# Another hand-written order for the first steps of a fused chunked attention and spatial-gating MLP

## The chip, the cores and the metric

The kernel runs on one core of one Trainium2 chip, in one launch. The metric is device time in microseconds (us), the median of several runs. The core has five engines that run side by side, each in its own program order: TensorE (PE, matmuls and transposes), VectorE (DVE), ScalarE (ACT), GpSimd (POOL) and SyncE (SP), which here only issues DMAs. In the profile PEld is PE's loading of weights.

## The reference

Four sequences (B = 4) of 768 tokens with 8 heads of 64 go through two blocks, everything in float32.

```python
# attention, per chunk of 32 queries; 8 memory keys, 16 keys to the left, 8 to the right
k_full = concat([mem_k, k[c_start-16 : c_end+8]]);  v_full likewise
a = softmax(q_c @ k_full.T / 8)
out[c] = a @ v_full
x = out as [B, 768, 512]
# gated MLP
h = gelu(x @ w_in)                      # w_in 512 x 1024
u, v = h[..., :512], h[..., 512:]
v_n = (v - mean(v)) / sqrt(var(v) + 1e-6) * g_ln
v_s = einsum('ts,bsd->btd', w_sg, v_n) + b_sg
out = x + (u * v_s) @ w_out
```

## The kernel before

The work is cut into 24 attention units (unit u is 128 tokens of one sequence, six units to a sequence) and, for each sequence, into MLP products. Large products take each operand as a high and a low part, so that one product is three groups of matmuls (`product`).

Every piece of work is a named step, and the string `ORDER` lists the steps. A loop goes through `ORDER` and lets each step issue its instructions. Since each engine keeps program order, `ORDER` is, read engine by engine, the queue of that engine; waits between engines follow from the data. Most steps run on a fixed engine; some can run on either of two, and a `*` behind the name takes the second one.

The names that matter here, with unit or part number behind them:

- `q`, `k`, `v`: loads of a unit's queries (256 KB, two buffers qa, qb), keys (368 KB, two buffers ka, kb) and values (512 KB, three buffers). A load into a buffer that an earlier unit used waits on SP until that unit's matmuls have read it, and everything behind it in SP's order waits too. `q2` and `k2` so wait for `S0`, `q3` and `k3` for `S1`, `q4` and `k4` for `S2`, `q5` and `k5` for `S3`, `q6` and `k6` for `S4`.
- `S`: 64 small matmuls for a unit's scores, into one PSUM tile `s` that all units share. `mx`, `sb`, `sm`, `sr` (DVE): row maximum, subtraction (which frees `s`), sum, reciprocal. `ex` (ACT): exponential. `nm` (DVE, `*` POOL): division, into the one tile `na`. `z`: clears what lies outside the sequence (POOL). `T`: four PE transposes of `na`; `p` (ACT, `*` DVE) copies them to SBUF as `pt`. `A`: 64 small matmuls with the values into one PSUM tile `av`. `xc`, `xh` (ACT) and `xl` (POOL or DVE): the result, its high and its low part.
- `ri13`, `ri12` and so on: loads of an eighth of w_in as raw 64-bit words (512 KB; raw buffers a to f). `d1` to `d6` decode them to float32 and split them: `d1` ACT, `d2` DVE (`*` ACT), `d3` and `d4` DVE, `d5` ACT (high part), `d6` POOL (`*` DVE, low part). `cb` loads g_ln and b_sg. `g`, `ga`, `gb`: load, high part, low part of a piece of w_sg; `ro` a quarter of w_out.
- `V`, `U`, `W`, `O`: the MLP's products on PE. `Va`, `Vb` are halves of a `V` for the first three units; `Vb00` needs `ri12`, `ri13` decoded and unit 0's high and low part. `v1` to `v9`, `u1` to `u4`, `w1` to `w4`, `o1` are the engines' work behind them.
- `zz4`: four matmuls of `ident` by `ident` into a free PSUM tile, whose result nobody reads. Each float32 matmul of `zz` shows as two MATMUL records, so `zz4` is eight, `zz1` two.

PE's order before begins: zz4 S0 S1 zz1 T0 S2 A0 S3 zz2 zz3 T1 zz1 Vb00 T2 S4 A1 Va00 T3 A2 Vb01 Va01 Vb02 S5 A3 T4. SP's order before begins: q1 q0 k0 k1 ri13 ri12 q2 k2 v0 ri11 q3 k3 q4 ri10 ri01 k4 v1 ri00 v2 ri02 cb k5 q5 v3 q6 k6 ri03.

Of the kernel before, what the change touches and what calls it, by code (L numbers as in the profile page):

```python
# [33 lines left out]


ORDER = """
zz4 q1 q0 k0 k1 S0 mx0 sb0 ex0 z0 sm0 sr0 nm0* S1 zz1 ri13 ri12 d1i12 d2i13* d1i13 q2 k2 mx1 sb1 T0 S2 ex1 v0
ri11 q3 k3 d2i12 d3i12 d4i12 sm1 d3i13 d5i12 p0 A0 mx2 sr1 sb2 nm1 d4i13 d6i12 S3 zz2 zz3 q4 ri10 ri01 k4 v1
T1 d2i11* d1i11 xh0 d3i11 d4i11 d5i13 ex2 d6i13 d5i11 xl0 mx3 sm2 sb3 sr2 nm2 zz1 Vb00 T2 S4 ri00 d6i11 d1i10
d2i10* ex3 p1 d2i01* xc0 d3i10 d4i10 A1 d3i01 d5i10 d1i01 d6i10 v2 ri02 cb k5 q5 v3 q6 k6 ri03 Va00 d2i00* xc1  # L40
xh1 d1i00 v100 sm3 sr3 p2* mx4 d3i00 d4i01 xl1* nm3* d4i00 v200 T3 A2 d5i01 xh2 sb4 xl2 d1i02 v300 d2i02* ex4
v400 sm4 v500 sr4 d3i02 vx00 Vb01 Va01 Vb02 xc2 p3 d5i00 v101 d6i01 cbh S5 v201 mx5 d6i00* sb5 A3 nm4* vy00
v600 T4 zz1 xc3 xh3 ex5 v301 d1i03 d2i03* p4* d4i02 z5 v401 sm5 d3i03 v700 v800 xl3 Va02 U001 S6 V03 d4i03
v900* mx6 v501 d5i03 u1001 v102 d5i02 v202 sb6 d6i03 d6i02 q7 k7 v4 g51 g11 g10 g21 q8 g20 g40 v302 u2001 sr5
u3001 ex6 vx01 nm5 vy01 v601 z6 A4 ga10 S7 xh4 ga21 ga51 u4001 mx7 v402 xl4 v701 ga20 v801 gb20* v502 sm6 sr6
gb21* vx02 U002 T5 p5 ga40 xc4 gb10 v901 v103 vy02 nm6* ga11 u1002 v203 u2002 v303 U003 u1003 u3002 sb7 v403
u4002 v503 v602 gb51 v702 gb40* V04 k8 q9 v5 A5 ex7 vx03 u2003 vy03 v603 S8 T6 g01 k9 ro0 ga01 xh5 p6 xl5
u3003 v802 v703 v803 v902 U000 V05 v903 xc5 v104 u4003 sm7 mx8 sb8 v204 gb01* sr7 v6 g50 S9 A6 g31 k10 q10
v105 ex8 nm7* gb11 ga31 gb31 v205 ga50 v305 gb50 d2o0 v405 g41 v7 v304 v404 g30 k11 U012 T7 sm8 mx9 v505 v504
sr8 vx05 u1000 ga41 gb41 p7 xc6 u1012 u2000 sb9 u3000 u2012 vx04 u4000 u3012 g00 v8 q11 U011 A7 S10 u4012 mx10  # L50
vy05 nm8* v605 ga30 v705 vy04 v604 T8 U013 U010 ga00 xc7 d3o0 v704 gb30* v804 v904 v805 ex9 d1o0 gb00* p8*
sb10 A8 S11 v905* sm9 u1010 u2010 u3010 u1011 ex10 d4o0 mx11 u2011 u4010 u3011 sm10 sr9 u4011 v9 q12 ro1 k12
k13 d2o1* d1o1 W001 d3o1 w1001 w2001 ro2 d5o0 W003 w1003 q13 W000 d4o1 d6o0* nm9* w2003 w1000 sb11 W002 w2000
sr10 d2o2 d3o2 w3003 ex11 d1o2 S12 w4003 w3001 xc8 w4001 z11 v10 ro3 v11 d4o2 w1002 w2002 d5o2 u1013 w3002
# [591 lines left out]
```

## Time and profile before

| | |
|---|---|
| median of 3 runs | 382.08 us (379.43 to 382.45) |
| profiled execution, its own time | 382.09 us |
| its span, first to last instruction | 380.3 us |
| PE busy | 365.1 us, 96% of the span |
| DVE, ACT, POOL busy | 254.2, 152.5, 120.1 us |
| DMA | 47.65 MB, mean 125 GB/s |

The profiled execution is as long as the median, and 1.8 us of it lie outside the span. Busy time says how long an engine had an instruction in it; what sets the end is read from the chain of waits and from the engines' timelines.

### The profile page before, as it was taken

To read this page: it belongs to the slowest core of one execution; us is meant where nothing else is said; L and a number is where in the kernel's file an instruction comes from. 1 tells how busy PE (TensorE), PEld (TensorE's weight loads), DVE (VectorE), ACT (ScalarE), POOL (GpSimd) and SP (SyncE) were. 2 spreads that over 40 slices of the span, in tenths; PEclk is the share of its full clock that TensorE was granted. 3 is DMA by queue.
4 is the path that set the end of the run, shared out by engine and by line. 5 is a ranking of instruction groups with operands and counts; after the bars stand their busy time and mean duration, and the time that the engine had idled before them with its cause. 6 is when DMAs were issued, how large, how long until landed. Compare 5 with 4: busy or idle time off the path is not lost.

```text
span 380.3 us, 11104 instructions
## 1 busy us (share of the span) xinstructions
PE 365.1 (96%) x4804; PEld 342.3 (90%) x4804; DVE 254.2 (67%) x472; ACT 152.5 (40%) x292; POOL 120.1 (32%) x144
## 2 busy tenths in 40 slices
PE   3698899999999999999999999999999999999996
PEld 3598788999998998899999888999999888999995
DVE  1988899997877868874545678766573347743642
ACT  1677686664314254540312254541221255531200
POOL 0255275622230333441402134731023055520210
PEclk9999999999999999999999999999999999999999
DMA  7998785845244533515111453204202300000033
GB/s 250 349 302 280 248 276 172 293 162 184 94 164 149 164 82 95 215 47 191 22 51 38 144 163 123 71 9 121 100 0 91 119 9 0 3 0 2 0 111 118
DMA packets 24528, 47.65 MB, mean 125 GB/s; under 512 B 4384, under 2 KB 13600, under 8 KB 24480
## 3 DMA queue, kind: packets, MB, share of 16 engines
q1 hardware_dynamic: 24480, 46.94, 37.4%
q8 instruction: 38, 0.62, 0.6%
q14 instruction: 10, 0.08, 0.1%
HBM read 36.96 MB, written 6.29 MB: 114 GB/s over the span
## 4 chain that ended last, share of the span: by engine, by line
PE 94%; DVE 3%; DMA 1%; issue 1%; SPq 0%; ACT 0%; POOL 0%; DVEq 0%
PE mmd L106 23%; PE mmc L106 22%; PE mma L106 21%; PE mmb L106 17%; PE av L106 7%; PE s L106 5%; DMA ka<-in_ks 1%; DVE ea L106 0%; DVE exc L106 0%; DVE rda L106 0%; SPq L106 0%; DVE rdb L106 0%; DVE mxa L106 0%; DVE mc L106 0%; DVE eb L106 0%
## 5 line engine op out<-in xcount | busy, mean ns | idle before, releaser
L106 DVE SCALAR_TENSOR_TENSOR mmd<-mmd,g_half,b_half 128x384 f32<-128x384 f32 x10 | 6.2, 622 | 16.8 <-PE mmd L106 16.8
L106 PE MATMUL mmc<-w_in_hi,paira 128*128 128x512 f32 (+1 forms) x56 | 14.2, 377 | 0.0
L106 PE MATMUL s<-ka,qa 64*32 64x64 f32 x768 | 10.9, 238 | 3.2 <-DMA ka<-in_ks 3.2
L106 PEld LDWEIGHTS s<-ka,qa 64*32 64x32 f32 x768 | 8.9, 112 | 5.0 <-issue 4.0
L106 DVE SCALAR_TENSOR_TENSOR mma<-mma,g_half,b_half 128x384 f32<-128x384 f32 x8 | 5.0, 624 | 12.6 <-PE mma L106 12.6
L106 PE MATMUL s<-kb,qb 64*32 64x64 f32 x768 | 10.9, 238 | 2.4 <-DVE ea L106 1.5
L106 PEld LDWEIGHTS s<-kb,qb 64*32 64x32 f32 x768 | 8.9, 112 | 4.5 <-DVE ea L106 1.8
L106 PEld LDWEIGHTS av<-pt,va 64*64 64x64 f32 x512 | 9.2, 145 | 3.7 <-issue 2.0
L106 PE MATMUL av<-pt,va 64*64 64x32 f32 x512 | 10.2, 229 | 2.3 <-issue 1.2
L106 DVE STREAM_TRANSPOSE y<-na 128x512 f32<-128x512 f32 x14 | 9.9, 706 | 2.9 <-POOL na L106 2.0
L106 ACT ACTIVATE ea<-ea 128x512 f32<-128x512 f32 x12 | 7.5, 625 | 10.0 <-DVE ea L106 10.0
L106 PEld LDWEIGHTS mmc<-w_in_hi,paira 128*128 128x128 f32 x56 | 10.0, 198 | 1.6
L106 POOL TENSOR_TENSOR pairb<-ue,pairb 128x384 fp32r<-128x384 f32 x3 | 3.1, 1017 | 25.6 <-ACT pairb L106 25.6
L106 PE MATMUL mmc<-w_in_hi,pairb 128*128 128x512 f32 x40 | 11.1, 399 | 0.0
L106 ACT ACTIVATE ga<-ga 128x512 f32<-128x512 f32 x12 | 7.6, 630 | 8.5 <-DVE ga L106 8.5
L106 PE MATMUL mmb<-paira,w_in_hi 128*128 128x384 f32 x56 | 10.9, 336 | 0.0
L106 DVE TENSOR_REDUCE mxa<-s 128x8 f32<-128x512 f32 x8 | 5.4, 681 | 7.8 <-PE s L106 7.8
L106 DVE SCALAR_TENSOR_TENSOR ga<-ga,mmc 128x512 f32<-128x512 f32 x12 | 8.2, 683 | 3.6 <-ACT ga L106 3.6
L106 PEld LDWEIGHTS av<-pt,vc 64*64 64x64 f32 x512 | 8.3, 134 | 2.0 <-issue 0.7
L106 PEld LDWEIGHTS av<-pt,vb 64*64 64x64 f32 x512 | 8.4, 134 | 1.9 <-issue 1.7
L106 POOL TENSOR_SCALAR rsa<-mva 128x1 f32<-128x1 f32 x8 | 1.8, 223 | 25.7 <-DVE mva L106 11.7
L106 ACT ACTIVATE gb<-gb 128x512 f32<-128x512 f32 x12 | 7.6, 632 | 5.8 <-DVE gb L106 5.8
(521 smaller groups left out, 1233.7 us busy)
## 6 DMA issues: line engine op xcount, KB each, us to landing
ka<-in_ks SPq DMA_DIRECT2D x12, 368.0 KB, 4.6
kb<-in_ks SPq DMA_DIRECT2D x12, 368.0 KB, 4.8
va<-in_vs SPq DMA_DIRECT2D x8, 512.0 KB, 5.0
vb<-in_vs SPq DMA_DIRECT2D x8, 512.0 KB, 4.9
vc<-in_vs SPq DMA_DIRECT2D x8, 512.0 KB, 4.9
pt<-y SPq DMA_DIRECT2D x112, 32.0 KB, 1.9
qb<-in_qs SPq DMA_DIRECT2D x12, 256.0 KB, 4.1
qa<-in_qs SPq DMA_DIRECT2D x12, 256.0 KB, 3.4
```

What stands on the lines that cost most here:

```text
L106: return self.tc.keep_in_program_order(getattr(self.engine, name)(*args, **kw))
```

## The change

The first 357 names of `ORDER` are put in another order; the rest of `ORDER` and all steps stay. Sixteen of these steps besides change sides between two engines. To POOL from DVE: nm1, nm5, gb20, gb21, gb40, gb01. To DVE from POOL: d6i13, d6i11, d6i10, xl3, gb10, gb50, v903. To ACT from DVE: d2i12, p4, d2o0.

PE's order then begins: zz1 S0 S1 S2 zz1 T0 zz4 A0 S3 zz3 zz2 T1 Vb00 T2 S4 A1 Va00 A2 T3 Va01 Vb01 Vb02 S5 A3 T4. SP's order begins: k0 q0 q1 k1 ri12 q2 k2 ri13 v0 ri11 q3 k3 q4 ri10 ri01 k4 q5 v1 v2 ri00 ri02 q6 cb k5 v3 ri03 k6.

```diff
--- before.py
+++ after.py
@@ -34,21 +34,21 @@
 
 
 ORDER = """
-zz4 q1 q0 k0 k1 S0 mx0 sb0 ex0 z0 sm0 sr0 nm0* S1 zz1 ri13 ri12 d1i12 d2i13* d1i13 q2 k2 mx1 sb1 T0 S2 ex1 v0
-ri11 q3 k3 d2i12 d3i12 d4i12 sm1 d3i13 d5i12 p0 A0 mx2 sr1 sb2 nm1 d4i13 d6i12 S3 zz2 zz3 q4 ri10 ri01 k4 v1
-T1 d2i11* d1i11 xh0 d3i11 d4i11 d5i13 ex2 d6i13 d5i11 xl0 mx3 sm2 sb3 sr2 nm2 zz1 Vb00 T2 S4 ri00 d6i11 d1i10
-d2i10* ex3 p1 d2i01* xc0 d3i10 d4i10 A1 d3i01 d5i10 d1i01 d6i10 v2 ri02 cb k5 q5 v3 q6 k6 ri03 Va00 d2i00* xc1
-xh1 d1i00 v100 sm3 sr3 p2* mx4 d3i00 d4i01 xl1* nm3* d4i00 v200 T3 A2 d5i01 xh2 sb4 xl2 d1i02 v300 d2i02* ex4
-v400 sm4 v500 sr4 d3i02 vx00 Vb01 Va01 Vb02 xc2 p3 d5i00 v101 d6i01 cbh S5 v201 mx5 d6i00* sb5 A3 nm4* vy00
-v600 T4 zz1 xc3 xh3 ex5 v301 d1i03 d2i03* p4* d4i02 z5 v401 sm5 d3i03 v700 v800 xl3 Va02 U001 S6 V03 d4i03
-v900* mx6 v501 d5i03 u1001 v102 d5i02 v202 sb6 d6i03 d6i02 q7 k7 v4 g51 g11 g10 g21 q8 g20 g40 v302 u2001 sr5
-u3001 ex6 vx01 nm5 vy01 v601 z6 A4 ga10 S7 xh4 ga21 ga51 u4001 mx7 v402 xl4 v701 ga20 v801 gb20* v502 sm6 sr6
-gb21* vx02 U002 T5 p5 ga40 xc4 gb10 v901 v103 vy02 nm6* ga11 u1002 v203 u2002 v303 U003 u1003 u3002 sb7 v403
-u4002 v503 v602 gb51 v702 gb40* V04 k8 q9 v5 A5 ex7 vx03 u2003 vy03 v603 S8 T6 g01 k9 ro0 ga01 xh5 p6 xl5
-u3003 v802 v703 v803 v902 U000 V05 v903 xc5 v104 u4003 sm7 mx8 sb8 v204 gb01* sr7 v6 g50 S9 A6 g31 k10 q10
-v105 ex8 nm7* gb11 ga31 gb31 v205 ga50 v305 gb50 d2o0 v405 g41 v7 v304 v404 g30 k11 U012 T7 sm8 mx9 v505 v504
-sr8 vx05 u1000 ga41 gb41 p7 xc6 u1012 u2000 sb9 u3000 u2012 vx04 u4000 u3012 g00 v8 q11 U011 A7 S10 u4012 mx10
-vy05 nm8* v605 ga30 v705 vy04 v604 T8 U013 U010 ga00 xc7 d3o0 v704 gb30* v804 v904 v805 ex9 d1o0 gb00* p8*
+k0 zz1 q0 q1 k1 S0 mx0 sb0 ex0 z0 sm0 S1 sr0 nm0* ri12 q2 k2 mx1 sb1 S2 zz1 ri13 v0 d1i12 d2i12* d3i12 d4i12
+d5i12 ex1 T0 zz4 mx2 sb2 sm1 sr1 d1i13 ex2 p0 A0 sm2 d2i13* d6i12 ri11 q3 k3 q4 S3 zz3 zz2 ri10 ri01 k4 q5 v1
+v2 ri00 d2i11* d3i13 d4i13 d3i11 d5i13 d1i11 xh0 d6i13* sr2 d4i11 xl0 nm1* d5i11 mx3 sb3 d2i10* d1i10 d2i01*
+T1 xc0 d3i10 d4i10 nm2 Vb00 T2 S4 d6i11* d5i10 p1 ex3 d1i01 d6i10* A1 ri02 q6 cb k5 v3 ri03 k6 Va00 xc1 xh1
+v100 d2i00* d1i00 sm3 d3i01 sr3 mx4 p2* sb4 nm3* xl1* d4i01 d3i00 d4i00 A2 d5i01 v200 T3 xh2 p3 v300 ex4 xl2
+Va01 Vb01 Vb02 d5i00 xc2 v101 v400 sm4 sr4 v500 v201 d1i02 d2i02* v301 S5 d6i01 cbh mx5 vx00 d6i00* A3 nm4*
+vy00 v600 T4 v401 sb5 d3i02 d2i03* d3i03 ex5 xc3 p4 xh3 d1i03 d4i02 v700 zz1 Va02 U001 S6 xl3* V03 d4i03 v501
+mx6 d5i02 v800 u1001 d5i03 v900* vx01 v102 q7 g50 g10 g20 v4 k7 d6i02 d6i03 sb6 u2001 u3001 v202 vy01 z5 sm5
+v601 v701 sr5 A4 v302 xh4 u4001 v402 nm5* v801 g21 v901 q8 ga10 ga20 ex6 gb20 z6 S7 U002 T5 xl4 mx7 gb10* sb7
+g40 g51 ga51 p5 v5 v7 k9 k8 U003 V04 g11 g41 q9 v6 v103 ga40 xc4 A5 S8 gb51 gb40 v203 v502 sm6 vx02 v303 u1003
+ga21 u1002 ga50 ex7 sr6 v403 u2003 u2002 u3002 u3003 vy02 nm6* v503 vx03 u4002 u4003 xh5 xl5 gb21 sm7 sr7 vy03
+v602 v603 U000 T6 v703 v702 gb50* xc5 ga41 ga11 v802 p6 v803 g31 V05 v902 mx8 sb8 v903* A6 S9 v105 v104 v205
+v305 v204 ro0 k10 g01 gb11 gb41 nm7* g30 q10 k11 v8 U012 mx9 v304 ga31 v404 v405 v504 T7 xc6 ga01 u1012 p7 ex8
+v505 sb9 vx05 sm8 sr8 vx04 gb01 gb31 u1000 q11 g00 U011 u2012 S10 A7 u2000 mx10 vy05 nm8* v605 ga30 u3012
+u4012 d2o0* u3000 u4000 v705 vy04 v604 T8 U013 U010 ga00 xc7 d3o0 v704 gb30* v804 v904 v805 ex9 d1o0 gb00* p8*
 sb10 A8 S11 v905* sm9 u1010 u2010 u3010 u1011 ex10 d4o0 mx11 u2011 u4010 u3011 sm10 sr9 u4011 v9 q12 ro1 k12
 k13 d2o1* d1o1 W001 d3o1 w1001 w2001 ro2 d5o0 W003 w1003 q13 W000 d4o1 d6o0* nm9* w2003 w1000 sb11 W002 w2000
 sr10 d2o2 d3o2 w3003 ex11 d1o2 S12 w4003 w3001 xc8 w4001 z11 v10 ro3 v11 d4o2 w1002 w2002 d5o2 u1013 w3002
```

## Rows read from the trace of the kernel before

**Rows 1.** The page, parts 1 and 4: busy time, share of the span and instructions of each engine; shares of the span in the chain of work that ended last.

```profile
PE 365.1 (96%) x4804; PEld 342.3 (90%) x4804; DVE 254.2 (67%) x472; ACT 152.5 (40%) x292; POOL 120.1 (32%) x144
...
PE 94%; DVE 3%; DMA 1%; issue 1%; SPq 0%; ACT 0%; POOL 0%; DVEq 0%
```

**Rows 2.** Busy time of each engine (and its instructions) in three stretches of the span, then the granted clock, the busy share of the DMA engines and GB/s.

```profile
10.00:20.00 10.00, 6.61 (x229) 5.29 (x214) 9.56 (x18) 6.45 (x12) 3.37 (x4) 1.00 0.97 351
...
40.00:160.00 120.00, 120.00 (x1954) 110.22 (x1948) 101.20 (x193) 62.69 (x123) 44.35 (x54) 1.00 0.55 179
...
160.00:380.00 220.00, 216.78 (x2121) 206.50 (x2119) 125.56 (x232) 68.23 (x133) 61.62 (x69) 1.00 0.21 66
```

**Rows 3.** PE's timeline, first half of the start: start and duration in us, line, operation, output and inputs, count; in brackets the idle time before it and what ended it.

```profile
6.54 1.17 PE L106 MATMUL s<-ka,qa 64*32 64x64 f32 x64 [3.05 <-DMA ka<-in_ks]
...
9.22 1.18 PE L106 MATMUL s<-kb,qb 64*32 64x64 f32 x64 [1.51 <-DVE ea L106]
...
13.62 1.17 PE L106 MATMUL s<-ka,qa 64*32 64x64 f32 x64 [0.20 <-DMA ka<-in_ks]
...
15.88 1.93 PE L106 MATMUL av<-pt,va 64*64 64x32 f32 x64 [1.08 <-DMA va<-in_vs]
...
18.74 1.17 PE L106 MATMUL s<-kb,qb 64*32 64x64 f32 x64 [0.93 <-DVE exb L106]
...
19.84 2.50 PE L106 MATMUL mmb<-ident 128*128 128x128 f32 x10
...
22.98 0.63 PE L106 MATMUL mmc<-ident 128*128 128x128 f32 x2
...
23.27 1.20 PE L106 MATMUL mmc<-w_in_hi,paira 128*128 128x256 f32 x4
...
24.27 0.95 PE L106 MATMUL mmc<-w_in_lo,paira 128*128 128x256 f32 x4
...
25.06 0.63 PE L106 MATMUL mmc<-w_in_hi,paira 128*128 128x256 f32 x4
...
26.05 0.86 PE L106 MATMUL s<-ka,qa 64*32 64x64 f32 x64
...
26.84 1.25 PE L106 MATMUL av<-pt,vb 64*64 64x32 f32 x64
```

**Rows 4.** SP's timeline: when a DMA was issued (start, duration of the issue). The lines are k0, ri12, v0, k3, v1 and k5.

```profile
1.63 0.43 SPq L106 DMA_DIRECT2D ka<-in_ks  x1
...
3.05 0.43 SPq L106 DMA_DIRECT2D rawc<-in_w_in  x1
...
8.60 0.43 SPq L106 DMA_DIRECT2D va<-in_vs  x1
...
10.81 0.87 SPq L106 DMA_DIRECT2D kb<-in_ks  x1
...
16.62 0.44 SPq L106 DMA_DIRECT2D vb<-in_vs  x1
...
26.57 0.38 SPq L106 DMA_DIRECT2D kb<-in_ks  x1
```

**Rows 5.** DMA issues, each line from a window of the span that holds the issue alone or nearly so: KB and us from issue to landing. In order: q1 (issued at 0.72), q0 (1.18), k0, ri12, v0, k3, v1, k5 (issue times of these six in rows 4) and k6 (28.86).

```profile
qb<-in_qs SPq DMA_DIRECT2D x1, 256.0 KB, 2.6
...
qa<-in_qs SPq DMA_DIRECT2D x1, 256.0 KB, 2.8
...
ka<-in_ks SPq DMA_DIRECT2D x1, 368.0 KB, 4.8
...
rawc<-in_w_in SPq DMA_DIRECT2D x1, 512.0 KB, 7.1
...
va<-in_vs SPq DMA_DIRECT2D x1, 512.0 KB, 7.1
...
kb<-in_ks SPq DMA_DIRECT2D x1, 368.0 KB, 7.8
...
vb<-in_vs SPq DMA_DIRECT2D x1, 512.0 KB, 7.4
...
kb<-in_ks SPq DMA_DIRECT2D x1, 368.0 KB, 6.7
...
ka<-in_ks SPq DMA_DIRECT2D x1, 368.0 KB, 8.9
```

**Rows 6.** DVE's timeline: the subtraction of unit 1, sb1, which frees the score tile for S2.

```profile
11.65 0.69 DVE L106 TENSOR_TENSOR eb<-s,mxb 128x512 f32<-128x512 f32 x1
```

**Rows 7.** PE's timeline, the two stretches in which it waited for nothing that the profile shows, and all matmuls between them.

```profile
35.85 0.52 PE L106 MATMUL mmd<-w_in_lo,paira 128*128 128x256 f32 x3 [1.06 <-issue]
36.20 0.63 PE L106 MATMUL mmd<-w_in_hi,paira 128*128 128x256 f32 x4
36.76 0.86 PE L106 MATMUL s<-kb,qb 64*32 64x64 f32 x64
37.55 1.02 PE L106 MATMUL av<-pt,va 64*64 64x32 f32 x56
39.79 0.32 PE L106 MATMUL av<-pt,va 64*64 64x32 f32 x8 [1.22 <-issue]
```

**Rows 8.** DMA queues in the stretches from 33 to 34 us and from 37 to 38 us: packets, MB and share of the 16 DMA engines of the queue that brings instructions.

```profile
q8 instruction: 1, 0.02, 6.2%
...
q8 instruction: 1, 0.02, 7.2%
```

## The prediction

> **What bounds the kernel now.** I read the page's busy times and its chain of waits first. PE is busy for 365.1 of 380.3 us and the chain that ended last lies on PE for 94% [rows 1]. So the kernel costs what PE has to do, plus 15.2 us in which it does nothing, plus what its early matmuls cost at the lower clock. The table by stretches then says where the idle time is: from 10 to 20 us PE is busy for 6.61 us, from 40 to 160 us throughout, and from 160 us on it lacks 3.2 us of 220 [rows 2]. The change touches none of the last. What it can win is before 24 us, in the two holes between 34 and 40 us (1.06 and 1.22 us [rows 7]), and nowhere else.
>
> PE's timeline shows what each early block waited for [rows 3]. S0 starts at 6.54, 0.1 us after k0 landed (1.63 + 4.8 = 6.43) [rows 4, 5]. A0 waits 1.08 us for v0 (8.60 + 7.1 = 15.7, start 15.88). S3 starts at 18.74; the profile names a decode step of DVE, but S3 reads none of it, and k3 landed at 10.81 + 7.8 = 18.6, so I put S3 down to k3. From S3 on PE runs without a gap until 34.8 us. The start is thus a train of loads, and PE takes over at S3.
>
> That train is full: between 10 and 20 us the DMA engines are 97% busy [rows 2], and a load that takes 2.6 us alone (q1) takes 7 to 8 when it queues [rows 5].
>
> The clock: the table says 1.00 in each stretch [rows 2], but durations say otherwise. Four 256-column matmuls take 0.95 us at 24.27 and 0.63 at 25.06; 64 score matmuls take 1.17 at 18.74 and 0.86 at 26.05 [rows 3]. So up to about 25 us PE ran at the lower of its two levels (1.2 GHz), and at the upper (2.4 GHz) behind it.
>
> **The loads of unit 0 in front.** Before k0 stood q1, 256 KB that S0 doesn't need. Its price lies between the step from q1's landing to q0's (1.18 + 2.8 less 0.72 + 2.6, 0.7 us) and its share at the pace of k0 (2.4 us from q0's landing for 368 KB, so 1.7 us for 256) [rows 5]. I take the middle, 1.1 us: S0 starts at 5.4. S1 and DVE's first steps move with it. S1 begins at 8.1 instead of 9.22 [rows 3], and sb1, which ended at 12.34 [rows 6], ends at 11.2.
>
> **The train behind it.** In the new order S2 comes next. It needs k2, which now has one w_in load less in front: between k0 (880 KB landed at 6.43) and ri12 (2272 KB at 10.15) the train moved 374 KB/us, so 512 KB are 1.4 us. S2 waited for k2 at 13.62, so it now starts at 12.2, or at 11.3 if k2 is still earlier. Then come S2 1.17, zz1 0.5, T0 1.0 and zz4 2.0 (0.25 a record [rows 3]), and A0 can begin at 16.0 to 16.9. It began at 15.88. v0 does not help: eight loads of the same sizes stand in front of it in either order, so with a full train it lands at 15.7 again. A0 takes 1.93, so PE is ready for S3 at 17.9 to 18.8. And k3 has the same eleven loads in front of it as before, so it lands at 18.6 again. S3 starts at 18.6 to 18.9 against 18.74. Here the 1.1 us won at S0 are spent; I book 0, from -0.3 to +0.2.
>
> **From S3 to the first product.** Before, PE did zz2, zz3, T1, zz1, Vb00; now zz3, zz2, T1, Vb00. One zz1 has gone ahead of S3, where it fills a wait. It took 22.98 to 23.27, so -0.3 us [rows 3]. What Vb00 needs lies earlier: A0 ends by 18.8, and its high part, its low part and the low parts of w_in are some 0.7 us each on ACT and DVE ([rows 6] has a full-width DVE operation at 0.69), so they are done by 21; Vb00 is due at 23.0. The 2 us between are the cover; without it each late us costs one.
>
> **Steps that change sides.** DVE gives up nine and takes seven, at no more than 0.69 each about 1.4 us less in all. POOL takes six and gives seven, ACT takes three. I cost this at nothing: DVE, ACT and POOL are busy 67, 40 and 32% [rows 1], and PE had no gap from 40 to 160 us [rows 2]. If the cover fails, the late step is nm1, now on POOL: T1 waits for it at most one POOL operation, about 1 us.
>
> **SP's queue.** q5 now stands before v1, v2 and ri00, and must wait until S3 has ended at 19.9. v1 was issued at 16.62 and landed at 24.0 [rows 4, 5]; now it is issued at 20.3, still behind a backlog that lasts to about 22.8, and gets 0.7 us of q5 in front, so 24.7. A1 wants it at 26.5 (26.84 before). Cover 1.8 us, cost 0. Likewise cb, k5 and v3 now wait behind q6, that is for the end of S4 at 26.5: k5 leaves at about 28.4 instead of 26.57. With k5's own 6.7 us it lands at 35.1, when S5 is due (36.76 less the first hole and 0.5); with the 8.9 us of k6, issued at 28.86, at 37.3. So 0 to +0.6 for S5; I take 0, since k5's own row is the nearest one, and the queue has lost the 256 KB of q5 by then.
>
> **The two holes.** PE stopped for 1.06 us before 35.85 and 1.22 before 39.79, with nothing to wait for; between the stops lie 127 matmuls with their weight loads, 254 instructions, and just before each end a 16 KB instruction load goes through the DMA engines [rows 7, 8]. So PE had run out of program, its next block being stuck behind data. In the new order the same number of matmuls precedes Vb02 and A3, so the stops fall at the same places. The first block comes as early as the DMA queue lets it, and with cb and k5 issued 2 us later the queue is shorter at the time: 0 to -1.06, I take -0.5. The second I leave, between -1.2 and +1. The Trainium skill (Runtime: NRT & Kernel Launch, Instruction fetch mechanics) says that programs arrive in 16 KiB blocks of 256 instructions, and that crossing into the next is mostly hidden; the trace agrees on the size and not on the hiding, and by the rule the term would be 0.
>
> Sum: 382.1 (the profiled execution, which is the median) - 0.3 - 0.5 = 381.3; with a small share of the DMA gaining, 381.2.
>
> **Rivals.**
> 1. The clock rises earlier. PE now works almost without a pause from S2 (12.2) on, before only from 18.74. If the upper level is there by S3, S3 saves 0.3, zz and T1 half of the 3.1 us from 19.84 to 22.98, and the first eight matmuls of Vb00 about 0.9: 2.8, less what then waits for the product's inputs at 21: some 2 us, so with the forecast's terms 379.2; with both holes gone too, 377.4. For it: activity is denser. Against: S and A use a part of the array, and between 18.74 and 24 dense work ran at the lower level all the same. The Trainium skill (TensorE: Matmul & The Clock Gate, Part 1) has the clock throttled by default and released by activity, which is this rival; the drop from 0.95 to 0.63 agrees.
> 2. Slower: the instruction block that PE enters about at Vb00 is late. (Counting back from the first hole 128 matmuls at a time, one comes to A1 and to the first matmuls of Vb00.) Before, it was there at 23.27. PE's program now runs ahead at the start and the loads after S3 are bunched (q5, v1, v2, ri00, ri02 in one row). A late block costs what the rows show, 1.06 to 1.22 a stop; with one at Vb00, one at A1, k5 late by 0.6 and the old holes kept: 382.1 - 0.3 + 2.3 + 0.6 = 384.7. It decides once a block needs more time than PE takes for the one before. Against: none stopped there before.
> 3. The loads don't do it: q0 and k0 land no earlier because first packets are slow whichever load they belong to, or everything is given back at k3 and at the holes: 382.1.
>
> **How the numbers follow.** Forecast (380.3 to 381.8) 0.40; rival 1 0.25, a good half of it above 378.3; rival 2 0.13, a third of it above 385.9; rival 3 0.22. A difference under 1%, 3.8 us, can hardly be told from no change here: the three runs alone span 3 us. Range 377.9 to 384.4, from rival 1 with one hole gone to most of rival 2. Faster than 378.3: 0.13; slower than 385.9: 0.05; same 0.82.
>
> **What would show it.** S0 near 5.4, A0 and S3 within 0.4 us of 15.9 and 18.7, k3's landing at 18.6: the train sets the start. Vb00 at 23.0 right behind T1. The holes 256 instructions apart, the first shorter. If the upper clock's durations show before 22 us, rival 1; if PE stops near Vb00 or A1 with nothing to wait for, rival 2. The prediction is wrong if the loads land in another rhythm (S3 by 17.5), or if PE waits for DVE or POOL between 40 and 110 us, where I saw no gap and costed none.

## The result, and the profile after

The changed kernel takes 384.88 us (median of 13 runs, 381.98 to 386.43) against 381.12 us (13 runs, 379.43 to 383.81): a ratio of 1.0072, 95% interval 1.0046 to 1.0097. It is slower, by 0.7% in this comparison; the medians as they stand are 1.0% apart. The profiled execution took 386.43 us with a span of 384.4, 4.1 us more than before; it is the slowest of the 13. The profile of one experiment further down, unit0_first_cb_late, was taken in a disturbed run and is not read.

The page first: busy time of the engines, and the chain that ended last by engine.

```profile
PE 365.9 (95%) x4804; PEld 343.0 (89%) x4804; DVE 253.3 (66%) x470; ACT 154.0 (40%) x295; POOL 118.5 (31%) x143
...
PE 90%; DMA 3%; DVE 3%; issue 2%; SPq 2%; ACT 1%; DVEq 0%; ACTq 0%
```

PE's own work has not grown (365.9 us against 365.1 [rows 1]), and the chain holds 90% of PE instead of 94. So time was lost by PE standing still or running slowly. PE's timeline of the changed kernel, start and duration in us, operation, count, and in brackets the idle time before it and what ended it:

```profile
4.58 1.17 PE L106 MATMUL s<-ka,qa 64*32 64x64 f32 x64 [2.36 <-DMA qa<-in_qs]
...
15.64 1.14 PE L106 MATMUL av<-pt,va 64*64 64x32 f32 x64
18.14 0.85 PE L106 MATMUL s<-kb,qb 64*32 64x64 f32 x64 [1.36 <-DVE exb L106]
...
21.72 0.33 PE L106 MATMUL mmb<-ident,na 128*128 128x128 f32 x1 [1.10 <-issue]
21.80 0.72 PE L106 MATMUL mmc<-w_in_hi,paira 128*128 128x256 f32 x4
...
25.01 0.90 PE L106 MATMUL av<-pt,vb 64*64 64x32 f32 x46
29.41 0.84 PE L106 MATMUL av<-pt,vb 64*64 64x32 f32 x18 [3.51 <-issue]
...
33.04 1.93 PE L106 MATMUL av<-pt,vc 64*64 64x32 f32 x64
...
41.65 0.86 PE L106 MATMUL s<-kb,qb 64*32 64x64 f32 x64
42.44 1.14 PE L106 MATMUL av<-pt,va 64*64 64x32 f32 x64
```

Against [rows 3] and [rows 7] the lines read as a ledger. S0 is 2.0 us earlier, S3 0.6, Vb00 1.47 (21.80 against 23.27), A1 1.83 (25.01 against 26.84). Up to there the change is a gain. (An idle time that "issue" ended is a stop in which PE waited for nothing that the profile shows; it is called a hole here.) Then PE stops after 46 of A1's 64 matmuls, for 3.51 us, with nothing to wait for. Behind that hole the same forms run at half the speed: A2 takes 1.93 us at 33.04, where A0 had taken 1.14. S5 starts at 41.65 instead of 36.76, 4.89 us late. The two holes that the kernel before had at Vb02 and A3 are gone, so A3 ends 3.5 us late (43.6 against 40.1), and that distance stays, with 0.6 us more by the end.

The stretches with their granted clock (busy us and instructions of PE, PEld, DVE, ACT, POOL, then the clock, the share of the DMA engines, GB/s):

```profile
15.30:28.90 13.60, 7.96 (x272) 6.86 (x270) 11.87 (x21) 8.05 (x15) 2.01 (x2) 1.00 0.94 352
28.95:39.15 10.20, 9.74 (x114) 9.38 (x115) 5.79 (x10) 6.54 (x12) 3.70 (x3) 0.50 0.53 193
39.20:160.00 120.80, 120.52 (x2078) 110.76 (x2077) 99.84 (x191) 62.96 (x123) 45.97 (x57) 1.00 0.54 175
```

From 28.95 to 39.15 us the clock is granted at 0.50, the lower level (1.2 GHz); before and behind it, at 1.00. The sum of the ledger at S5: -1.83 (lead at A1) + 3.51 (hole) - 1.06 (hole of before that is gone) leaves 0.62; the rest of the 4.89, 4.3 us, is what ten microseconds at the lower clock cost. From the hole's end PE takes 12.2 us to S5; before, from the same matmul on (at about 27.7 us, see below), it took 8.0 without the hole at Vb02.

Which load went where: SP's issues around S3 in the changed kernel (q5, v1, v2, ri00, ri02), and the queue that brings instructions in the tenth of a us from 27.1.

```profile
19.01 0.33 SPq L106 DMA_DIRECT2D qb<-in_qs  x1
19.39 1.26 SPq L106 DMA_DIRECT2D vb<-in_vs  x1
20.69 0.43 SPq L106 DMA_DIRECT2D vc<-in_vs  x1
21.17 0.43 SPq L106 DMA_DIRECT2D rawe<-in_w_in  x1
22.25 0.33 SPq L106 DMA_DIRECT2D rawa<-in_w_in  x1
```

```profile
q8 instruction: 1, 0.02, 62.5%
```

Five loads, 2.3 MB, leave within 3.6 us after S3, right when PE enters the block of its program that holds Vb00 to the middle of A1 (21.72). The block behind that one starts through the DMA engines only at 27.1 us, and 2.3 us later PE goes on.

In the kernel before, the same block started at 25.1 us:

```profile
q8 instruction: 1, 0.02, 59.9%
```

With 2.3 us more it was there at 27.4, and PE had done 46 matmuls of A1 at about 27.7 (an estimate: 46/64 of A1's 1.25 us from 26.84 [rows 3]). So the kernel before had no more than 0.3 us to spare at this place. In the changed kernel PE is there 1.8 us earlier (25.9) and the block starts 2.0 us later; 1.8 + 2.0 - 0.3 is the hole of 3.5 us. Half of the hole is PE's lead, half is the late block.

### The profile page after: what moved, and what is told of

Its sections match the earlier page's. It is cut to its first block, busy times and chain, and to the rows that moved or that the text cites. A ratio compares the mean times of both kernels' runs of the same rounds, so it can differ in the third digit from the quotient of the medians.

```text
span 384.4 us, 11107 instructions
## 1 busy us (share of the span) xinstructions
PE 365.9 (95%) x4804; PEld 343.0 (89%) x4804; DVE 253.3 (66%) x470; ACT 154.0 (40%) x295; POOL 118.5 (31%) x143
## 4 chain that ended last, share of the span: by engine, by line
PE 90%; DMA 3%; DVE 3%; issue 2%; SPq 2%; ACT 1%; DVEq 0%; ACTq 0%
PE mmb L106 22%; PE mmd L106 20%; PE mmc L106 20%; PE mma L106 16%; PE av L106 7%; PE s L106 5%; SPq L106 2%; DMA ka<-in_ks 1%; DMA qa<-in_qs 1%; DMA pt<-y 0%; DVE xb L106 0%; DVE exd L106 0%; DVE md L106 0%; DVE ea L106 0%; DVE mxc L106 0%
## 5 line engine op out<-in xcount | busy, mean ns | idle before, releaser
L106 DVE SCALAR_TENSOR_TENSOR mmb<-mmb,g_half,b_half 128x384 f32<-128x384 f32 x10 | 6.2, 622 | 16.5 <-PE mmb L106 16.5
L106 DVE SCALAR_TENSOR_TENSOR mmd<-mmd,g_half,b_half 128x384 f32<-128x384 f32 x8 | 5.0, 625 | 12.4 <-PE mmd L106 12.4
L106 PE MATMUL av<-pt,vb 64*64 64x32 f32 x512 | 9.7, 223 | 3.5 <-issue 3.5
L106 PE MATMUL mmb<-w_in_hi,pairb 128*128 128x512 f32 x40 | 11.2, 402 | 0.0
L106 POOL TENSOR_TENSOR pairb<-ug,pairb 128x384 fp32r<-128x384 f32 x3 | 3.1, 1026 | 25.5 <-ACT pairb L106 25.5
L106 PEld LDWEIGHTS av<-pt,vc 64*64 64x64 f32 x512 | 9.1, 145 | 2.0 <-issue 1.2
L106 POOL TENSOR_SCALAR rsa<-mva 128x1 f32<-128x1 f32 x8 | 2.1, 266 | 27.1 <-DVE mva L106 12.9
L106 DVE SCALAR_TENSOR_TENSOR gb<-gb,mmc 128x512 f32<-128x512 f32 x12 | 8.2, 683 | 3.3 <-ACT gb L106 3.2
L106 ACT COPY xa<-av 128x512 f32<-128x512 f32 x9 | 5.2, 581 | 12.5 <-PE av L106 12.5
L106 PE MATMUL av<-pt,vc 64*64 64x32 f32 x512 | 10.0, 230 | 0.0
L106 ACT ACTIVATE eb<-eb 128x512 f32<-128x512 f32 x12 | 7.6, 633 | 5.5 <-DVE eb L106 3.0
```

What stands on the lines that cost most here:

```text
L106: return self.tc.keep_in_program_order(getattr(self.engine, name)(*args, **kw))
```

## The experiments

Theory 1: the block of PE's program that PE needs in A1 is asked for when PE enters the block before it, and comes through the DMA engines behind the data that is queued there; the moved loads made that queue longer, and the idle time then took the clock down. Theory 2: a block takes its 5 to 6 us in any case, and PE, with its lead, came too early.

**Two loads behind ri02.** The changed kernel with

```diff
-q5 v1 v2 ri00 ri02 q6 cb k5
+q5 v1 ri02 v2 ri00 q6 cb k5
```

> The changed kernel with two loads moved: v2 and ri00 go behind ri02 in SP's order, so that they are issued after 22.2 us instead of at 20.7 and 21.2; nothing else differs. Theory 1 (backlog: the block of PE's program that is asked for when PE enters the block before, at 21.7 us, comes through the DMA engines only behind the data that was issued before that moment): the data ahead of it is now q5 and v1, which land at 24.3, instead of all up to ri00, about 26.9; the block's 16 KB start at 24 to 25 us instead of 27.1, the hole in A1 shrinks from 3.5 us to 0.5 to 1.3, the clock stays at its upper level, and the time is 379.5 to 381.5. Theory 2 (the block needs its time whatever data is queued, and PE came too early): hole 3 to 3.6 us, clock falls to half for about 10 us, 384 to 386.

Measured 385.68 us, ratio to the kernel before 1.0104 (1.005 to 1.0158). PE around A1, SP's issues and the block:

```profile
20.99 0.33 PE L104 MATMUL mmb<-ident,na 128*128 128x128 f32 x1 [1.85 <-issue]
...
25.40 0.90 PE L104 MATMUL av<-pt,vb 64*64 64x32 f32 x46
29.34 0.84 PE L104 MATMUL av<-pt,vb 64*64 64x32 f32 x18 [3.05 <-issue]
```

```profile
17.90 0.43 SPq L104 DMA_DIRECT2D vb<-in_vs  x1
21.61 0.33 SPq L104 DMA_DIRECT2D rawa<-in_w_in  x1
21.99 0.43 SPq L104 DMA_DIRECT2D vc<-in_vs  x1
22.46 0.43 SPq L104 DMA_DIRECT2D rawe<-in_w_in  x1
```

```profile
q8 instruction: 1, 0.02, 60.4%
```

The hole is 3.05 us and the block starts at 26.9. Theory 1 as I had put it falls: at the moment when PE entered the block (20.99) only q5 and v1 were queued, and they had landed by 23.0 (17.90 + 5.1). But theory 2 isn't shown either, though hole and time lie in its ranges, since ri02, v2 and ri00 left 0.6 to 1.5 us behind that moment; if the request itself needs about a microsecond to reach the queue, they are in front of it all the same. I mended theory 1 that way.

**One load behind ri02.** The changed kernel with `v2 ri02 ri00` instead of `v2 ri00 ri02`.

> The changed kernel with one load moved: ri00 behind ri02, issued after 22.2 us instead of at 21.2. Theory 1 (backlog): the data ahead of the block ends with v2, which lands at 25.6, so the block's 16 KB start at about 25.8 us, and the hole in A1 is 1.8 to 2.6 us, between that of the changed kernel (3.5) and that of the kernel with v2 moved as well; the clock may fall or not: 380.5 to 384. Theory 2 (own latency): hole 3 to 3.6 us, 384 to 386.

Measured 384.51 us, ratio 1.0075 (1.0039 to 1.0111); PE entered the block at 21.38, the next started at 26.8, and the hole in A1 was 3.78 us. Again no shrinking, as theory 2 has it, and for the same reason inconclusive: both loads left within 0.9 us of PE's entry.

**q5 alone in the kernel before.**

```diff
-q4 ri10 ri01 k4 v1 ri00 v2 ri02 cb k5 q5 v3
+q4 ri10 ri01 k4 q5 v1 ri00 v2 ri02 cb k5 v3
```

> The kernel before with one load moved: q5 from behind k5 to in front of v1, where the changed kernel has it, so that v1, ri00 and v2 wait for the end of S3 and are issued at about 20.3 to 21.6 us instead of 16.6 to 17.7. Theory 1 (backlog): PE enters the block before A1's at 23.2 us with data queued that lands at about 27.3 instead of 26.6, the block comes 0.5 to 2 us later, a hole opens in A1 that the kernel before does not have: 0.3 to 2 us, time 381.3 to 383 and above that if the clock falls. Theory 2 (PE ahead): PE is no earlier than before, no hole in A1, 380.5 to 381.5.

Measured 382.7 us, ratio 1.003 (0.9996 to 1.0063).

```profile
24.55 0.90 PE L104 MATMUL av<-pt,vb 64*64 64x32 f32 x46
28.66 0.85 PE L104 MATMUL av<-pt,vb 64*64 64x32 f32 x18 [3.22 <-issue]
```

The profiled run, the slowest of the 12, has the hole of the changed kernel, at the same place, 3.22 us, which the profiled run of the kernel before doesn't have. It isn't the moved load's alone, since this execution too was two us ahead at A1 (24.55 against 26.84): its block started at 26.3 us, 1.2 later than before, and the rest is the lead. The time lies in the range of theory 1, but the interval touches 1, so a loss from q5 alone isn't shown in the old order.

**Unit 0's loads alone in the kernel before.**

```diff
-zz4 q1 q0 k0 k1 S0
+zz4 k0 q0 q1 k1 S0
```

> The kernel before with only the first four loads in the new order: k0 q0 q1 k1 instead of q1 q0 k0 k1. S0 starts at 4.6 instead of 6.54. If the train of loads sets the start, A0 stays at 15.9 and S3 within 0.5 us of 18.7, the clock rises at about 25 us as before, and the time is that of before, 380.5 to 381.5. If the early loads alone make PE run ahead of its program (as in the changed kernel), a hole opens near A1 and the time is 383 or more.

Measured 380.67 us, ratio 0.9979 (0.9944 to 1.0013).

```profile
16.30 1.17 PE L104 MATMUL s<-kb,qb 64*32 64x64 f32 x64 [0.75 <-DMA kb<-in_ks]
...
20.84 1.20 PE L104 MATMUL mmc<-w_in_hi,paira 128*128 128x256 f32 x4
...
38.82 0.36 PE L104 MATMUL av<-pt,va 64*64 64x32 f32 x8 [2.96 <-issue]
```

S3 starts at 16.30, 2.4 us earlier than before, so the train of loads does move, against my step. The lead is given back at 38.82: a hole of 2.96 us in A3 instead of the 1.22 of before. The hole at Vb02 is gone, and none opens in A1. The time is the same within what is measured.

**Loads behind q6.** The changed kernel with

```diff
-q5 v1 v2 ri00 ri02 q6 cb k5
+q5 v1 q6 v2 ri00 ri02 cb k5
```

> The changed kernel with v2, ri00 and ri02 behind q6, which waits for the end of S4 at about 24.7 us, so that after q5 and v1 nothing is issued for five us. Theory 1, mended (the block's 16 KB go behind all data that is issued up to about 1 us after PE has entered the block before, at 21.5 us): ahead of it lie only q5 and v1, which land by 24.3; the 16 KB start at 22.8 to 24 us instead of 27.1; no hole in A1, or one under 0.7 us; the clock stays up there; A2 may wait up to 1 us for v2. Time 379 to 381.5, unless a later block gives it back as in before_unit0_first. Theory 2 (the block takes its 5 to 6 us in any case): hole 3 us or more, 384 or more.

Measured 384.46 us, ratio 1.007 (1.0043 to 1.0097).

```profile
26.22 0.90 PE L104 MATMUL av<-pt,vb 64*64 64x32 f32 x46
27.51 0.53 PE L104 MATMUL av<-pt,vb 64*64 64x32 f32 x18 [0.39 <-issue]
...
30.64 1.14 PE L104 MATMUL av<-pt,vc 64*64 64x32 f32 x64 [1.00 <-DVE mf L104]
...
37.40 0.74 PE L104 MATMUL mmd<-w_in_hi,paira 128*128 128x256 f32 x4 [2.24 <-DVE paira L104]
```

```profile
q8 instruction: 1, 0.02, 66.6%
```

Nothing is issued here between v1 at 19.99 and q6 at 26.32, and the block starts at 24.9 instead of 27.1: the hole in A1 is 0.39 us. That bears out the mended theory 1, though the block came a microsecond later than I had said. Not all of the shrinking is the block's, as PE came to A1 1.2 us later than in the changed kernel (26.22 against 25.01): in this execution the clock was at the lower level from 17.7 to 24.5 us. The time isn't won, and 379 to 381.5 was wrong: v2 landed at 30.5 (26.70 + 3.8), so A2 waits 1.00 us, and Vb02 waits 2.24 for what follows from it, with the lower clock again from 38.1 to 41.6.

**q5 back behind k5.** The changed kernel with

```diff
-ri10 ri01 k4 q5 v1 v2 ri00 ri02 q6 cb k5 v3
+ri10 ri01 k4 v1 v2 ri00 ri02 q6 cb k5 q5 v3
```

> The changed kernel with q5 behind k5, where the kernel before has it, so that v1, v2 and ri00 no longer wait for the end of S3 and are issued at about 14.6 to 16 us. Theory 1, mended: between 16 and 22 us nothing is issued, the block asked for at about 21.5 us goes behind ri00 alone, which lands at about 25 to 26, and starts at 23 to 25 us instead of 27.1: hole in A1 0 to 1.5 us, clock up, 379.5 to 381.5. Theory 2: hole 3 us or more, 384 or more.

Measured 381.74 us, ratio 1.0002 (0.9976 to 1.0029).

```profile
21.31 0.33 PE L104 MATMUL mmb<-ident,na 128*128 128x128 f32 x1 [1.12 <-issue]
...
24.35 0.90 PE L104 MATMUL av<-pt,vb 64*64 64x32 f32 x46
27.66 0.53 PE L104 MATMUL av<-pt,vb 64*64 64x32 f32 x18 [2.41 <-issue]
```

```profile
q8 instruction: 1, 0.02, 66.4%
```

PE enters the block at 21.31, as early as in the changed kernel (21.72), and the next block starts at 25.1 instead of 27.1. So the loads set when the block comes, at the same lead: theory 2, that it takes its time whatever is queued, falls. The hole is 2.41 us, more than I expected, as PE was also faster through S4 (A1 at 24.35); the block itself came when it came before (25.1), so this hole is the lead. I had the clock stay up, but in this execution, the slowest of the ten, it was at the lower level from 29.3 to 36.1 us. The time is that of the kernel before: in the new order this one load's place is worth the whole loss.

**Va00 in front of A1.** The changed kernel with PE's `S4 Va00 A1` instead of `S4 A1 Va00`.

> The changed kernel with Va00 in front of A1 on PE: twelve dense matmuls of 1.4 us come before the 64 small ones in which the hole opens; loads unchanged. By both theories the block still arrives at about 29.4 us, and PE gets to its end about 1.4 us later with that work done: hole 2.0 to 2.4 us. If the clock falls as before, 383 to 384.5; if the shorter hole leaves it up, 380 to 382.

Measured 383.15 us, ratio 1.004 (1.001 to 1.0069).

```profile
26.02 0.77 PE L104 MATMUL av<-pt,vb 64*64 64x32 f32 x34
29.42 0.66 PE L104 MATMUL av<-pt,vb 64*64 64x32 f32 x30 [2.63 <-issue]
```

PE stops after 34 matmuls of A1 instead of 46: the 12 matmuls of Va00 went in front, and the stop came 12 matmuls sooner. The place of the hole is counted in instructions of the program, not in data. The block is no earlier (PE goes on at 29.42), so the hole is 2.63 us, and the time lies where I had put it for a clock that falls. It fell for less long, from 31.5 to 34.9 us, and once before the hole, from 17.8 to 21.2.

**cb late.** The kernel before with unit 0's loads in front (before_unit0_first) and, beside that, cb moved from behind ri02 to behind ro0 and cbh behind v903.

> The kernel with the first four loads in the new order (before_unit0_first) and cb, 384 KB that nobody reads before 90 us, issued at about 53 us behind ro0 instead of at 23 us; its halving on POOL moves behind v903. In before_unit0_first the block behind A3 started at 36.5 us, one us before the last queued load landed, and the hole was 3.2 us. Theory 1: without cb, which took the DMA engines almost 4 us, that queue ends at about 34, the block comes before PE needs it, the hole is under 1 us, the clock stays up: 377 to 379. Theory 2: the hole stays at 3 us and the time at 380 to 381.

Measured 380.61 us, ratio 0.9961 (0.9928 to 0.9995), a little faster than the kernel before; less than theory 1 promised (377 to 379), and in the range of theory 2 (380 to 381). Whether the hole in A3 shrank isn't shown. (That hole is 2.96 us in the trace of before_unit0_first, not 3.2.)

**Three moves in the new order.** The changed kernel with q5 behind k5, A1 behind Va00, cb behind k8 and cbh behind v902.

> The changed kernel with three moves: q5 behind k5, A1 behind Va00, and cb (384 KB that nobody reads before 90 us) behind k8, its halving behind v902. Theory (PE runs out of program because the next block queues behind data, and the idle time then costs it the upper clock): the block starts at about 25.2 us as in q5_behind_k5 and is there at 27.6; PE reaches the end of the block before at about 26.4 instead of 25.0, with twelve dense matmuls done; hole in A1 0.8 to 1.5 us instead of 2.4; the lower clock lasts 0 to 3.4 us instead of 6.8; the blocks behind come on time without cb in their way. 378 to 380.5. If the hole is not set by the loads and the place of A1: 381 to 383, like q5_behind_k5.

Measured 381.4 us, ratio 0.9974 (0.9946 to 1.0003).

```profile
21.11 0.33 PE L104 MATMUL mmb<-ident,na 128*128 128x128 f32 x1 [1.16 <-issue]
...
27.50 0.66 PE L104 MATMUL av<-pt,vb 64*64 64x32 f32 x30 [0.44 <-issue]
28.86 1.14 PE L104 MATMUL av<-pt,vc 64*64 64x32 f32 x64 [0.69 <-ACT xa L104]
...
37.45 0.32 PE L104 MATMUL av<-pt,va 64*64 64x32 f32 x8 [0.60 <-issue]
```

The hole in A1 shrinks to 0.44 us and the one in A3 to 0.60, and the granted clock of the run is 1.000. The holes do what theory 1 says; the time, which I had put at 378 to 380.5, is 381.4, in the range that I gave for the case that they don't: the stop of 1.16 us in T1 and a wait for unit 1's result at A2 are left.

**Three moves in the old order.** The kernel before with k0 q0 q1 k1, cb behind ro0 (cbh behind v903) and A1 behind Va00.

> The kernel before with the first four loads in the new order, cb behind ro0 (halving behind v903) and A1 behind Va00; all else as before. Theory: the block that PE wants in A1 is there at about 25.6 us, and with Va00 done first PE gets there at about 25.9: no hole, or one under 0.5 us; no hole in A3 either, as cb is out of the way; the upper clock from about 21 us on without a break. 377 to 379.5, the fastest of all. If A1's hole does not matter there: 380.6, like unit0_first_cb_late.

Measured 380.88 us against 381.87 of the kernel before beside it, ratio 0.9946 (0.9914 to 0.9978): faster than both kernels, though by 0.5% only: I had put it at 377 to 379.5.

```profile
16.99 1.19 PE L104 MATMUL s<-kb,qb 64*32 64x64 f32 x64 [0.87 <-DVE ea L104]
...
26.24 0.74 PE L104 MATMUL mmc<-w_in_lo,paira 128*128 128x256 f32 x4 [0.58 <-POOL w_in_lo L104]
...
37.30 0.32 PE L104 MATMUL av<-pt,va 64*64 64x32 f32 x7 [0.46 <-issue]
```

A1 has no hole, A3 one of 0.46 us. The second line shows a new wait: Va00, being earlier, waits 0.58 us for a low part of w_in on POOL.

**What is left of the change.** The changed kernel with q5 behind k5 and the first four loads as before.

> The changed kernel with q5 behind k5 and with the first four loads as before (q1 q0 k0 k1): what is left of the change is the order of the other steps and their change of sides. S0 starts at about 6.5 us again, PE is some 0.5 to 1 us later at T1 and meets its program blocks with as much more cover. If the head start only runs into the hole, the time is that of q5_behind_k5 and of the kernel before, 381 to 382.3; if the loads of unit 0 in front are worth something of their own, 382.5 to 383.5; if the new order of the steps is worth something and only the head start spoils it, 379.5 to 380.8.

Measured 383.98 us, ratio 1.0039 (1.001 to 1.0068). S3, which waits for k3, and the DMA engines from 8 to 10 us, first of this kernel, then of the kernel before:

```profile
20.34 0.89 PE L104 MATMUL s<-kb,qb 64*32 64x64 f32 x64 [1.58 <-DMA kb<-in_ks]
```

```profile
8.00:10.00 2.00, 0.49 (x39) 0.25 (x32) 1.38 (x2) 0.18 (x1) 0.00 (x0) 1.00 0.44 116
```

```profile
8.00:10.00 2.00, 0.78 (x58) 0.78 (x63) 1.14 (x2) 0.63 (x1) 0.11 (x1) 1.00 0.86 285
```

S3 starts at 20.34, 1.6 us later than before. The new order puts ri13 behind q2, which must wait for S0; so five loads instead of six leave at once, and with S0 late they are through before q2 may go: 116 GB/s from 8 to 10 us instead of 285. The loads of unit 0 in front hide that, since S0 then ends at 5.8. The late S3 isn't all. This execution, the slowest of its 12, stops in A1 too, and the clock is at the lower level from 31.3 to 38.1 us:

```profile
29.75 0.53 PE L104 MATMUL av<-pt,vb 64*64 64x32 f32 x18 [1.76 <-issue]
```

So without q5 and without unit 0's loads the order of the other steps costs some 0.4%. By the ratios unit 0's loads in front give back 0.4% in the new order (1.0039 to 1.0002) and gave 0.2% in the old one (0.9979); the intervals overlap in the first case and hold 1 in the second, so neither is clear of the noise.

## Why the prediction was wrong

The time, 384.88, lies above my range (377.9 to 384.4), and the sign is rival 2's. The step that failed is the 0 for q5 in SP's queue, with the clock's fall that no term held.

- **What bounds the kernel, and where it can change:** right. All that moved lies before 44 us; from there the distance to the kernel before stays within 0.6 us.
- **Loads of unit 0:** the term was too small. k0 landed at 3.6 (0.72 + 2.9) and S0 started at 4.58, a gain of 2.0 us where I took 1.1 (the middle of 0.7 and 1.7 is 1.2). What it waited for at the end was q0, now behind k0: the profile names qa.
- **The train behind it:** half right. A0 came at 15.64 (I had 16.0 to 16.9) and S3 at 18.14 (18.6 to 18.9). Of the 2.0 us 0.6 was left, not 0. That the train of loads is fixed was my error; before_unit0_first, with S3 at 16.30, shows how far it moves when the first loads are freed earlier. (The 2.6 us of q1 beside the 7 to 8 of later loads set 256 KB against 368 and 512, so not all of that difference is queueing.)
- **From S3 to the first product:** the clock did what rival 1 said. A0 takes 1.14 us at 15.64 instead of 1.93 [rows 3], and Vb00 started at 21.80, although PE stopped 1.1 us in T1 for want of program. Rival 1 came true up to A1, and rival 2 behind it.
- **SP's queue:** here the prediction failed. I costed q5 in front of v1 at 0 because v1 would still land before A1 reads it, and it did. I asked of a moved load only who reads the data, not what else goes through the same DMA engines. q5_behind_k5 shows that in the new order this one step is worth the whole difference (1.0002 instead of 1.0072): the block behind A1's first half starts at 25.1 us instead of 27.1.
- **The two holes:** the term (-0.5) was mis-sized and misplaced. I took the stops' places from where the kernel before had stopped. The traces' stops up to 44 us lie 127 matmuls, or twice that, apart, and whichever block comes late stops PE; in the changed kernel that was T1 (1.10 us) and A1 (3.51), and at Vb02 and A3 the blocks came in time, because PE was now slow. I had counted back to these places (to within a few matmuls), but only for rival 2.
- **Rival 2:** the mechanism and the place were right (a late block at Vb00 and A1), its time of 384.7 too, by luck: I priced a stop at 1.06 to 1.22 us from the rows of before and gave it 0.13. The hole was three times as long, and the clock's fall behind it, 4.3 us, was in no term. Against it I had held that no block stopped there before. I had read the instruction loads at the two holes alone [rows 8] and didn't ask how much time the other blocks had to spare: at A1 it was 0.3 us.
- **Steps that change sides:** no wait of T1 for nm1 shows, so the 0 stands for that one; the rest's order was not free, as the last experiment shows (1.0039). Its late loads and its hole in A1 are seen in the trace; how much each costs isn't shown.

The Trainium skill (Runtime: NRT & Kernel Launch, Instruction fetch mechanics) has the crossing into a new block mostly hidden; here, with the DMA engines 94% busy in the stretch before it (15.30 to 28.90 us), it cost 3.51 us, and the measurement decides.

What stays open: how the DMA engines choose between a program block and queued data. loads_behind_q6 and q5_behind_k5 show that fewer loads in front bring the block sooner; in the first two experiments the block is late although two or three loads left only behind PE's entry; the rule between them was only argued. When a block is asked for isn't seen either: "when PE enters the block before" is theory 1's assumption. That idle time in the hole lowers the clock is read from the order of events in the traces (lower from 28.95, in the last half us of the hole; never lower between 17.4 and 378 us in the profiled run of order_three_moves, whose longest hole was 1.16 us), not from an experiment that keeps the hole and leaves the clock. What decides it is open, too: loads_behind_q6 and va00_before_a1 went to the lower level at 17.7 and 17.8 us, around a wait of 1.4 us at S3, and the changed kernel, with 1.36 us there, didn't.

## What to carry to other kernels

A hand-ordered kernel of small matmuls consumes its own program fast: here 127 matmuls with their weight loads lie between two stops, which is some 2 us of small ones (64 take 0.9 to 1.25 at the upper clock), and the next block shares the DMA engines with the data. When a load is moved, ask what program block must come at that time and how much time it has to spare. Large matmuls, not small ones, where the engines are full of data, make a block last longer; va00_before_a1 points that way (hole 2.63 instead of 3.51 us), though its interval overlaps that of the changed kernel. A lead of PE is worth nothing if it ends in a stop that also costs the upper clock.

## What the hardware showed that I had not expected

A block of program (0.02 MB in its queue's row) needed several us from PE's entry into the block before until its transfer began: 3.8 in q5_behind_k5 (21.31 to 25.1), 5.4 in the changed kernel (21.72 to 27.1), 5.9 in v2_ri00_behind_ri02 (20.99 to 26.9). That isn't a fixed delay. The block that the changed kernel needs in A3, at 43.3 us, started at 37.6, three us before PE got to the end of the block it was in (40.7, 127 matmuls from 29.41):

```profile
q8 instruction: 1, 0.02, 82.8%
```

And from 270 to 380 us, where the DMA engines are 13% busy, each block starts 1 to 5 us before PE enters the one in front of it (counting 127 matmuls to a block). So a block can be asked for that early, and where loads are queued it comes later.

The lower clock outlasts the hole by far and by different amounts: in the changed kernel 10.2 us, although PE was busy for 9.74 of them, in ri00_behind_ri02, whose hole was longer (3.78), 3.4 us (29.6 to 33.0). The changed kernel's 13 runs go with their mean granted clock: 381.98 us for the one at 0.996, 382.06 to 384.61 for the four at 0.991, 383.94 to 386.43 for the five at 0.986 and 0.987, 384.88 to 386.13 for the three at 0.981 and 0.982. The run with the highest clock is within 0.9 us of the median of the kernel before.
